# One core, attention into a spectral MLP: a searched order of work and loads, and DMA transposes for part of x and u

## The chip, the cores and the metric

The kernel runs on 1 core of one Trainium2 chip. The metric is device microseconds of one execution; the span of the profile is about 2 us shorter than the time. There is one core, so the state of a run is judged by its time alone: a run more than 1.5% above the fastest of the same kernel counts as slow and is left out of a ratio.

## The reference

Eight batches of chunked attention (8 heads, 576 positions, head size 64, softmax within chunks of 64) give x; then a gated token mixer and a residual MLP. Cut to what matters:

```python
scores = q_c @ k_c.T / 8                 # per chunk of 64
attn = softmax(scores)                   # within the chunk
x = (attn @ v_c)                         # [8, 576, 512], heads side by side
theta = x @ w_theta
y = w_tok_r @ (x * cos(theta)) + w_tok_i @ (x * sin(theta))   # over positions
u = x + y
out = u + relu(u @ w_ch)                 # float32
```

## The kernel before

Batches go in pairs (p = 0 to 3), each of 9 tiles of 128 positions, in 5 groups g of two tiles (group 2, the middle one, has one). Everything is emitted in an order written down as a list of items: `a1` turns q and k, `a2` scores and exp, `a3` attention times v and division, `a4` turns x, `a5` theta with cos and sin, `z` their products with x, `y` the token product (one per batch and 128 channels, plus the residual x, which gives u transposed, `uT`), `w` the last product, `st` the final sum and the store. Each engine does its instructions in that order.

```python
def a4(p, g, bits):                       # x -> xT, on TensorE
    ps = psum2("ps_xT", FP16)
    ...
    for jj in range(n):
        for db in range(NDB):             # NDB = 4
            nc.tensor.transpose(psv[:, db, jj*P : jj*P+P],
                                st[p]["x", g][:, jj, db*P : db*P+P], id16)
    ...                                   # then one copy PSUM -> xT on DVE or ACT

def w(p, j):
    for db in range(NDB):
        nc.tensor.matmul(ps[:, 0:DM], uT[:, db, j*P : j*P+P], wch16[:, db, :], ...)
        nc.tensor.matmul(ps[:, DM+db*P : DM+db*P+P],     # u turned back
                         uT[:, db, j*P : j*P+P], id16)
    nc.scalar.activation(out=r, in_=ps[:, 0:DM], func=AF.Relu)

def out_tile(p, j):
    nc.vector.tensor_tensor(out=o, in0=ps[:, DM : 2*DM], in1=r, op=ALU.add)
    nc.sync.dma_start(out[...], o[...])
...
# loads: on GpSimd's queue, each as soon as its buffer's last reader has been emitted
```

PSUM is one ring of four buffers; a tile of `w` holds one until its `st`.

The softmax here doesn't subtract the row's maximum and nothing guards it: scores larger than these inputs give would overflow.

Of the kernel before, what the change touches and what calls it, by code (L numbers as in the profile page):

```python
# [9 lines left out]
FP32 = mybir.dt.float32  # L10
FP16 = mybir.dt.float16
# [38 lines left out]


# [1 line left out]
def kernel(  # L53
# [27 lines left out]
    GROUPS = [(0, 2), (2, 2), (4, 1), (5, 2), (7, 2)]  # L81
    VP = D + 2
    NAT = 7

    const = ctx.enter_context(tc.tile_pool(name="const", bufs=1))
    glob = ctx.enter_context(tc.tile_pool(name="glob", bufs=1))
# [102 lines left out]
            nc.gpsimd.dma_start(wnat[hf][ri][0:CH, 2, :], ap[KT * P : S, :])  # L189

    def load_w(ap, f16):
        nc.gpsimd.dma_start(f16, ap.rearrange("(a p) e -> p a e", p=P))


# [143 lines left out]
            op=ALU.mult,  # L338
        )

    def a4(p, g, bits):

        j0, n = GROUPS[g]
        ps = psum2("ps_xT", FP16)
        psv = ps[:, 0 : NDB * n * P].rearrange("p (a s) -> p a s", a=NDB)
        for jj in range(n):
            for db in range(NDB):
                nc.tensor.transpose(  # L348
                    psv[:, db, jj * P : jj * P + P],
                    st[p]["x", g][:, jj, db * P : db * P + P],  # L350
                    id16,
                )
# [12 lines left out]

    def a5(p, g):

# [99 lines left out]
            op=ALU.add,  # L467
        )

    def w(p, j):  # L470

        uT = uT_tile(p)
        ps = psum2("ps_uw")
        for db in range(NDB):
            nc.tensor.matmul(  # L475
                ps[:, 0:DM],
                uT[:, db, j * P : j * P + P],
                wch16[:, db, :],
                start=(db == 0),
                stop=(db == NDB - 1),  # L480
            )
            nc.tensor.matmul(  # L482
                ps[:, DM + db * P : DM + db * P + P],
                uT[:, db, j * P : j * P + P],
                id16,
            )
        r = outp.tile([P, DM], FP32, name="relu", bufs=3)
        nc.scalar.activation(out=r, in_=ps[:, 0:DM], func=AF.Relu)  # L488
        st[p]["w", j] = (ps, r)

    def out_tile(p, j):
        ps, r = st[p].pop(("w", j))
        o = outp.tile([P, DM], FP32, name="o32")
        nc.vector.tensor_tensor(out=o, in0=ps[:, DM : 2 * DM], in1=r, op=ALU.add)  # L494
# [52 lines left out]
_INS = ['q', 'k', 'v', 'moe_w_theta', 'moe_w_tok_r', 'moe_w_tok_i', 'moe_w_ch']  # L547
# [26 lines left out]
```

## Time and profile before

| | before |
|---|---|
| time, median of 4 runs | 219.27 us (218.46 to 222.02) |
| span of the profile | 217.4 us |
| TensorE / VectorE / ScalarE / GpSimd busy | 91 / 61 / 54 / 39% |
| first theta matmul; end of the last matmul | 21.75; 213.1 us |
| TensorE busy between these two | 188.5 of 191.4 us |
| after the last matmul | 4.3 us |

In the lines below, PEld is TensorE's loading of weights, and SPq and POOLq are the DMA issues of SP (SyncE) and GpSimd. A row of a stage gives the stretch, its length, then busy microseconds (and instructions) of PE, PEld, DVE, ACT and POOL, the granted clock of TensorE, the share of the DMA engines and GB/s. Busy time of matmuls overlaps, so the cost of one in a stream is read from the distance of two starts. The lines that carry this are in the prediction.

### The profile page before, as it was taken

How to read it: one execution, taken by the hardware profiler on the slowest of the kernel's cores; microseconds unless marked ns; L12 is line 12 of the kernel's file. 1: busy time of each engine (PE TensorE's matmuls, PEld its weight loads, DVE VectorE, ACT ScalarE, POOL GpSimd, SP SyncE). 2: the span in 40 equal slices, each digit the busy share in tenths (PEclk: the TensorE clock that was granted, in tenths of full speed). 3: DMA queues.
4: the chain of work that ended last, by engine and by line, in shares of the span. 5: the costliest groups of instructions: out<-in, count | busy, mean ns of one | idle time of the engine just before them, and what ended most of it. 6: DMA issues, size and time to landing. Idle time of an engine off the chain costs nothing.

```text
span 217.4 us, 6721 instructions
## 1 busy us (share of the span) xinstructions
PE 198.8 (91%) x2994; PEld 138.8 (64%) x2994; DVE 132.8 (61%) x230; ACT 118.5 (54%) x138; POOL 85.1 (39%) x118
## 2 busy tenths in 40 slices
PE   0485999989999999999997999999999999999992
PEld 0374568765677875667886664776766675777750
DVE  0148486747977575869776837567836655275273
ACT  2244484338968689838574468753085446321242
POOL 7896468679885698765920000000000000000000
PEclk9999999999999999999999999999999999999999
DMA  6999999999999999999990012112121313113136
GB/s 59 177 131 166 200 181 179 177 170 132 166 221 196 165 132 181 213 228 192 142 164 5 3 48 72 51 51 48 53 96 51 121 48 100 48 49 147 48 124 216
DMA packets 83612, 26.92 MB, mean 124 GB/s; under 512 B 76288, under 2 KB 78976, under 8 KB 83584
## 3 DMA queue, kind: packets, MB, share of 16 engines
q0 software_dynamic: 77696, 16.54, 86.0%
q1 hardware_dynamic: 5888, 9.96, 13.5%
q8 instruction: 23, 0.38, 0.7%
q14 instruction: 5, 0.04, 0.0%
HBM read 33.06 MB, written 9.44 MB: 195 GB/s over the span
## 4 chain that ended last, share of the span: by engine, by line
PE 80%; DMA 6%; DVE 4%; POOL 3%; issue 3%; ACT 2%; POOLq 0%
PE ps_y L455 28%; PE ps_theta L377 14%; PE ps_uw L475 13%; PE ps_qkT L266 6%; PE ps_y L434 4%; PE ps_sT L292 4%; DMA wtheta<-in_moe_w_theta_dram 3%; PE ps_uw L482 3%; PE ps_xT L348 3%; PE ps_x L320 3%; DMA qk<-in_k_dram 3%; POOL v L176 2%; PE ps_wT L218 1%; POOL qk L155 1%; DVE o L494 1%
## 5 line engine op out<-in xcount | busy, mean ns | idle before, releaser
L455 PE MATMUL ps_y<-wT,z 128*128 128x288 f16 x448 | 59.8, 286 | 1.2 <-issue 1.2
L455 PEld LDWEIGHTS <-z 128*128 128x128 f16 x448 | 42.2, 98 | 13.8 <-issue 1.5
L176 POOL DMA_DIRECT2D v<-in_v_dram x56 | 42.0, 766 | 17.3 <-DMA qk<-in_k_dram 10.7
L475 PE MATMUL ps_uw<-wch,uT 128*128 128x512 f16 x144 | 42.5, 380 | 0.0
L488 ACT ACTIVATE relu<-ps_uw 128x512 f32<-128x512 f32 x36 | 21.6, 600 | 37.6 <-PE ps_uw L482 37.2
L463 DVE TENSOR_TENSOR uT<-ps_y,xT 128x576 f16<-128x576 f32 x28 | 21.2, 755 | 28.8 <-PE ps_y L455 28.7
L494 DVE TENSOR_TENSOR o<-ps_uw,relu 128x512 f32<-128x512 f32 x36 | 24.5, 686 | 11.7 <-ACT relu L488 11.5
L482 PE MATMUL ps_uw<-id,uT 128*128 128x128 f16 x144 | 31.5, 219 | 0.0
L377 PE MATMUL ps_theta<-wtheta,xT 128*128 128x512 f16 x128 | 30.5, 384 | 0.1
L266 PE MATMUL ps_qkT<-id,qk 128*64 128x128 f16 (+1 forms) x640 | 22.5, 227 | 6.4 <-DMA qk<-in_q_dram 5.7
L387 ACT ACTIVATE cos<-ps_theta,pihalf 128x1024 f16<-128x1024 f32 (+1 forms) x20 | 20.6, 1029 | 12.7 <-PE ps_theta L377 12.4
L334 DVE TENSOR_TENSOR x<-ps_x,recip 128x512 f16<-128x512 f32 x36 | 24.9, 691 | 1.2
L266 PEld LDWEIGHTS <-qk 128*64 128x64 f16 (+1 forms) x640 | 19.1, 118 | 8.8 <-DMA qk<-in_q_dram 5.7
L299 ACT ACTIVATE eT<-ps_sT 128x1024 f16<-128x1024 f32 (+1 forms) x20 | 18.3, 940 | 11.4 <-PE ps_sT L292 11.4
L475 PEld LDWEIGHTS <-uT 128*128 128x128 f16 x144 | 14.1, 98 | 14.7
L197 DVE COPY kT<-ps_qkT 128x1024 f16<-128x1024 f16 (+1 forms) x13 | 15.2, 1169 | 12.5 <-ACT qT L199 12.5
L155 POOL DMA_DIRECT2D qk<-in_k_dram x24 | 19.1, 797 | 5.5 <-DMA qk<-in_q_dram 2.9
L377 PEld LDWEIGHTS <-xT 128*128 128x128 f16 x128 | 12.1, 99 | 13.6 <-issue 0.9
L155 POOL DMA_DIRECT2D qk<-in_q_dram x24 | 19.3, 805 | 2.1 <-POOLq L558 0.8
L391 ACT ACTIVATE sin<-ps_theta 128x1024 f16<-128x1024 f32 (+1 forms) x20 | 18.7, 933 | 0.0
L199 ACT COPY kT<-ps_qkT 128x1024 f16<-128x1024 f16 (+1 forms) x7 | 8.4, 1224 | 14.2 <-DVE qT L197 14.2
L292 PE MATMUL ps_sT<-qT,kT 64*64 64x64 f16 x576 | 12.3, 223 | 3.9 <-ACT kT L199 2.9
(51 smaller groups left out, 212.0 us busy)
## 6 DMA issues: line engine op xcount, KB each, us to landing
out_dram<-o SPq DMA_DIRECT2D x32, 256.0 KB, 2.1
qk<-in_q_dram POOLq DMA_DIRECT2D x16, 256.0 KB, 6.9
qk<-in_k_dram POOLq DMA_DIRECT2D x16, 256.0 KB, 8.2
v<-in_v_dram POOLq DMA_DIRECT2D x40, 64.0 KB, 6.4
v<-in_v_dram POOLq DMA_DIRECT2D x16, 128.0 KB, 6.3
out_dram<-o SPq DMA_DIRECT2D x8, 128.0 KB, 2.9
wnat<-in_moe_w_tok_r_dram POOLq DMA_DIRECT2D x2, 288.0 KB, 8.9
wnat<-in_moe_w_tok_i_dram POOLq DMA_DIRECT2D x2, 288.0 KB, 9.6
```

The costliest lines, as they stand in the source:

```text
L155: nc.gpsimd.dma_start(t[(pp // 2) : (pp // 2) + m // 2, ti].rearrange("p h t d -> p h (t d)"), src.rearrange("h (p t) d -> p h (t d)", t=2),)
L176: nc.gpsimd.dma_start(v16[pp : pp + m, sl, :, 0:D], v[2 * p + bb, :, s0 : s0 + m, :].rearrange("h s d -> s h d"),)
L266: nc.tensor.transpose(psv[par * D : par * D + D, w, e, tk, 0:rows], t[0:rows, w, 2 * e + par, tk, :], id16[0:rows, 0:rows],)
L292: nc.tensor.matmul(psv[kh * CH : kh * CH + CH, par, i, e, :], kT[par * D : par * D + D, e, c0 : c0 + CH], qT[par * D : par * D + D, e, c0 ...
L334: nc.vector.tensor_tensor(out=xo, in0=px[:, :, :, 0:D], in1=recip.broadcast_to((P, 2, NE, D)), op=ALU.mult,)
L377: nc.tensor.matmul(ps[:, jj * DM : jj * DM + DM], xt[:, db, :], wtheta16[:, db, :], start=(db == 0), stop=(db == NDB - 1),)
L455: nc.tensor.matmul(psv[:, hf, 0:HS], zt[:, db * P : db * P + P], wT[:, kt, hf * HS : hf * HS + HS], start=(kt == 0), stop=(kt == 2 * KT),)
L463: nc.vector.tensor_tensor(out=uT_tile(p)[:, db, sl].rearrange("p (f c) -> p f c", f=2), in0=psv[:, :, 0:HS], in1=xT_tile(p)[:, db, sl].rea ...
L475: nc.tensor.matmul(ps[:, 0:DM], uT[:, db, j * P : j * P + P], wch16[:, db, :], start=(db == 0), stop=(db == NDB - 1),)
L482: nc.tensor.matmul(ps[:, DM + db * P : DM + db * P + P], uT[:, db, j * P : j * P + P], id16,)
L488: nc.scalar.activation(out=r, in_=ps[:, 0:DM], func=AF.Relu)
L494: nc.vector.tensor_tensor(out=o, in0=ps[:, DM : 2 * DM], in1=r, op=ALU.add)
```

## The change

Its intent: TensorE is the bound, and the DMA engines are four fifths idle once the loads are done, so turn there what can be turned by DMA, and search an order of all work, loads and choices of engine that fits. The core of the diff, the list of items left out (the two comment lines at its end say in words what it does there; KT is 4: tiles 0 to 3 of a pair go with its first batch, 4 to 8 with its second):

```diff
+    U_DMA = 3
...
+    def xt(p, g):
...
+        for jj in range(n):
+            c0 = x_col(j0 + jj)
+            nc.sync.dma_start_transpose(xT[:, :, c0 : c0 + P], x[:, jj, :])
...
     def a4(p, g, bits):
+        if bits & 16:
+            xt(p, g)
+            if n == 1:
+                xm_copy(p, bits >> 1)
+            return
...
+    def ut(p, bb, db):
+        cols = slice(KT * P, T) if bb else slice(0, KT * P)
+        nc.sync.dma_start_transpose(
+            un_tile(p, bb)[:, :, db * P : db * P + P], uT_tile(p)[:, db, cols]
+        )
...
     def w(p, j):
-            nc.tensor.matmul(ps[:, DM + db * P : DM + db * P + P], uT[...], id16)
-        nc.scalar.activation(out=r, in_=ps[:, 0:DM], func=AF.Relu)
+            if 2 * p + int(j >= KT) < U_DMA:
+                nc.tensor.matmul(ps[:, DM + db * P : DM + db * P + P], uT[...], id16)
+        if 2 * p + int(j >= KT) < U_DMA:
+            nc.scalar.activation(out=r, in_=ps[:, 0:DM], func=AF.Relu)
...
     def out_tile(p, j, bits):
+        else:
+            nc.vector.scalar_tensor_tensor(out=o, in0=ps[:, 0:DM], scalar=0.0,
+                in1=un_tile(p, int(j >= KT))[...], op0=ALU.max, op1=ALU.add)
+        eng = nc.gpsimd if bits & 2 else nc.sync
...
-    # loads issued by a rule between the items
+    # loads are items of the order (lq, lv, lw, lt, lc)
```

The 33 transposes (13 of x in the last 7 groups, 20 of u of the last five batches) all go through SP's queue; 18 of the 36 tiles are stored from GpSimd's queue instead of SP's.

More of the change, by code (lines that the diff above doesn't have):

```diff
@@ L19 @@
 ORDER = """
-a1.0.0:0 a2.0.0:0 a1.0.1:3 a1.0.2:2 a3.0.0.0:0 a2.0.1:0 a3.0.0.1:0 a2.0.2:0 a3.0.2.0:0
-a4.0.0:1 a4.0.2:3 a3.0.1.0:0 a3.0.1.1:0 a5.0.2:0 a4.0.1:1 a5.0.0:0 z.0.2.0:0 z.0.0.0:0
-tw.0.1:0 tw.1.0:0 a5.0.1:0 z.0.0.1:0 tw.0.2:0 tw.1.1:0 z.0.1.0:0 z.0.1.1:0 tw.0.0:1
-tw.1.2:0 a1.0.3:2 yh.0.0:0 a2.0.3:0 yh.0.1:0 a1.0.4:3 a3.0.3.0:0 yh.1.0:0 a3.0.3.1:0
-a2.0.4:0 yh.1.1:0 a3.0.4.0:0 a1.1.0:0 a4.0.3:0 w.0.0:0 a2.1.0:0 a3.0.4.1:0 st.0.0:0
-a5.0.3:0 a4.0.4:1 a1.1.1:2 z.0.3.0:0 a5.0.4:0 a3.1.0.0:0 w.0.1:0 z.0.4.0:0 a1.1.2:0
@@ L26 @@
-st.0.1:0 z.0.3.1:0 w.0.2:0 st.0.2:0 a3.1.0.1:0 a2.1.1:0 z.0.4.1:0 a1.1.3:3 w.0.3:0
-a4.1.0:1 st.0.3:0 y.0.1.0:0 a2.1.2:0 a2.1.3:0 a3.1.1.0:0 a5.1.0:0 a3.1.3.0:0 a1.1.4:2
-y.0.1.1:0 a3.1.2.0:0 a2.1.4:0 y.0.1.2:0 a4.1.2:0 a1.2.0:1 a3.1.1.1:0 a1.2.1:0 z.1.0.0:0
-y.0.1.3:0 a4.1.1:0 a3.1.4.0:0 a2.2.1:0 a2.2.0:0 a3.1.3.1:0 w.0.4:0 z.1.0.1:0 a5.1.2:0
-st.0.4:0 a4.1.3:1 w.0.5:0 a5.1.1:0 st.0.5:0 a3.1.4.1:0 a1.2.2:3 z.1.2.0:0 a5.1.3:0
-z.1.1.0:0 w.0.6:0 a4.1.4:1 w.0.7:0 st.0.6:0 st.0.7:0 a1.2.3:3 z.1.1.1:0 a3.2.1.0:0
@@ L32 @@
-a1.2.4:0 w.0.8:0 a5.1.4:0 st.0.8:0 y.1.0.0:0 a2.2.2:0 a2.2.3:0 z.1.4.0:0 a3.2.1.1:0
-z.1.3.0:0 z.1.3.1:0 y.1.0.1:0 a3.2.2.0:0 a2.2.4:0 a1.3.0:3 z.1.4.1:0 y.1.0.2:0 a4.2.1:1
-a4.2.2:0 a1.3.1:1 a3.2.0.0:0 a3.2.4.0:0 y.1.1.0:0 a1.3.2:3 a2.3.0:0 a3.2.0.1:0 a1.3.3:3
-a2.3.1:0 a3.3.0.0:0 y.1.0.3:0 a4.2.0:0 a3.2.3.0:0 a1.3.4:3 a3.2.3.1:0 a3.2.4.1:0
-y.1.1.1:0 w.1.0:0 st.1.0:0 a4.2.3:0 a4.2.4:1 a5.2.0:0 y.1.1.2:0 w.1.1:0 a5.2.2:0
-z.2.0.0:0 a5.2.1:0 st.1.1:0 z.2.2.0:0 z.2.0.1:0 w.1.2:0 a5.2.3:0 z.2.1.0:0 z.2.1.1:0
@@ L38 @@
-st.1.2:0 a5.2.4:0 y.1.1.3:0 w.1.3:0 a2.3.2:0 z.2.3.0:0 z.2.3.1:0 st.1.3:0 a3.3.1.0:0
-y.2.0.0:0 z.2.4.0:0 a2.3.3:0 a3.3.1.1:0 a2.3.4:0 y.2.0.1:0 a4.3.1:0 w.1.4:0 z.2.4.1:0
-a3.3.0.1:0 st.1.4:0 a3.3.4.0:0 y.2.0.2:0 w.1.5:0 a3.3.4.1:0 st.1.5:0 a3.3.3.0:0
-y.2.1.0:0 a3.3.3.1:0 a3.3.2.0:0 y.2.1.1:0 w.1.6:0 a4.3.2:3 w.1.7:0 st.1.6:0 a5.3.2:0
-w.1.8:0 st.1.7:0 y.2.0.3:0 st.1.8:0 a5.3.1:0 w.2.0:0 a4.3.0:1 z.3.1.0:0 st.2.0:0 w.2.1:0
-st.2.1:0 z.3.1.1:0 y.2.1.2:0 a5.3.0:0 w.2.2:0 z.3.2.0:0 a4.3.4:0 st.2.2:0 z.3.0.0:0
@@ L44 @@
-z.3.0.1:0 y.2.1.3:0 a4.3.3:0 w.2.3:0 y.3.0.0:0 w.2.4:0 st.2.3:0 st.2.4:0 a5.3.4:0
-a5.3.3:0 w.2.5:0 z.3.4.0:0 z.3.4.1:0 st.2.5:0 y.3.0.1:0 w.2.6:0 y.3.0.2:0 z.3.3.0:0
-w.2.7:0 st.2.6:0 z.3.3.1:0 y.3.0.3:0 st.2.7:0 w.2.8:0 y.3.1.0:0 w.3.0:0 st.2.8:0
-st.3.0:0 y.3.1.1:0 w.3.1:0 y.3.1.2:0 st.3.1:0 w.3.2:0 y.3.1.3:0 st.3.2:0 w.3.3:0 w.3.4:0
-w.3.5:0 st.3.3:0 st.3.4:0 w.3.6:0 w.3.7:0 st.3.5:0 w.3.8:0 st.3.6:0 st.3.7:0 st.3.8:0
+lq.0.0:0 a1.0.0:2 lq.0.2:0 a1.0.2:2 lq.0.1:0 a2.0.0:0 a2.0.2:0 a1.0.1:3 lv.0.2:0
@@ new lines @@
+lv.0.0:0 a3.0.0.0:0 a3.0.2.0:0 a2.0.1:0 a3.0.0.1:0 lv.0.1:0 a3.0.1.0:0 lw.0:0 lq.0.3:0
+a3.0.1.1:0 a4.0.0:1 a4.0.2:0 lq.0.4:0 a4.0.1:1 a5.0.2:0 lt.0.1:0 z.0.2.0:0 a5.0.0:0
+lt.0.0:0 z.0.0.0:0 a1.0.3:3 a5.0.1:0 lq.1.0:0 a1.0.4:0 z.0.1.0:0 lv.0.4:0 tw.0.2:0
+tw.0.0:0 z.0.1.1:0 lt.1.0:0 z.0.0.1:0 tw.0.1:0 a2.0.3:0 lt.1.1:0 a2.0.4:0 lv.0.3:0
+lv.1.0:0 a1.1.0:2 yh.0.0:0 lq.1.2:0 a3.0.4.0:0 a2.1.0:0 a3.0.4.1:0 yh.0.1:0 a4.0.4:1
+lc.0:0 tw.1.1:0 tw.1.2:1 tw.1.0:1 a3.0.3.0:0 lq.1.1:0 a3.0.3.1:0 a5.0.4:0 lv.1.2:0
@@ new lines @@
+a4.0.3:1 yh.1.0:0 lq.1.3:0 a5.0.3:0 z.0.4.0:0 lq.1.4:0 a3.1.0.0:0 z.0.3.0:0 a1.1.2:2
+yh.1.1:0 z.0.3.1:0 z.0.4.1:0 a2.1.2:0 lv.1.3:0 a3.1.0.1:0 a1.1.1:3 lv.1.1:0 w.0.0:0
+st.0.0:0 y.0.1.0:0 a3.1.2.0:0 a1.1.3:0 lq.2.0:0 w.0.1:0 lv.1.4:0 a4.1.2:1 st.0.1:0
+y.0.1.1:0 a2.1.3:0 a1.1.4:3 a2.1.1:0 a3.1.3.0:0 lq.2.2:0 w.0.2:0 st.0.2:0 y.0.1.2:0
+a2.1.4:0 a3.1.3.1:0 a4.1.0:1 a5.1.2:0 lv.3.0:0 a3.1.1.0:0 a1.2.0:2 a5.1.0:0 lq.2.1:0
+lv.2.2:0 a3.1.4.0:0 lv.2.0:0 a3.1.1.1:0 y.0.1.3:0 a4.1.1:1 a3.1.4.1:0 z.1.0.0:0 a1.2.2:1
@@ new lines @@
+w.0.3:0 st.0.3:0 a4.1.3:1 a4.1.4:0 lq.2.3:0 z.1.2.0:0 a5.1.1:0 w.0.4:0 a5.1.4:0 st.0.4:2
+w.0.5:0 lq.2.4:0 z.1.1.0:0 z.1.0.1:0 z.1.4.0:0 a5.1.3:0 st.0.5:0 z.1.1.1:0 a2.2.0:0
+a1.2.1:2 y.1.0.0:0 lv.2.1:0 a1.2.3:1 a3.2.0.0:0 lv.2.4:0 z.1.3.0:0 a2.2.2:0 y.1.0.1:0
+z.1.3.1:0 a2.2.1:0 lv.3.2:0 a3.2.2.0:0 a1.2.4:0 w.0.6:0 st.0.6:0 a4.2.2:1 lv.2.3:0
+y.1.0.2:0 w.0.7:0 z.1.4.1:0 a3.2.0.1:0 lq.3.0:0 a2.2.4:0 st.0.7:2 lv.3.4:0 y.1.0.3:0
+a3.2.1.0:0 a3.2.4.0:0 y.1.1.0:0 a4.2.0:0 a3.2.4.1:0 a1.3.0:3 a2.2.3:0 lq.3.2:0
@@ new lines @@
+a3.2.1.1:0 w.0.8:0 lq.3.1:0 lq.3.3:0 a5.2.2:0 a4.2.1:0 lv.3.3:0 w.1.0:0 lq.3.4:0
+st.0.8:0 lv.3.1:0 z.2.2.0:0 st.1.0:0 y.1.1.1:0 a5.2.1:0 w.1.1:0 st.1.1:2 a5.2.0:0
+z.2.1.0:0 z.2.0.0:0 y.1.1.2:0 a3.2.3.0:0 a1.3.2:0 z.2.1.1:0 a2.3.0:0 a1.3.1:0 z.2.0.1:0
+w.1.2:0 st.1.2:0 y.1.1.3:0 y.2.0.0:0 ut.1.1.0:0 a2.3.2:0 ut.1.1.3:0 a3.3.0.0:0 a1.3.3:0
+a3.2.3.1:0 y.2.0.1:0 a4.2.4:16 a4.2.3:17 a2.3.1:0 a3.3.0.1:0 a1.3.4:0 a2.3.3:0
+a3.3.1.0:0 ut.1.1.2:0 y.2.0.2:0 a3.3.1.1:0 a4.3.0:17 a2.3.4:0 ut.2.0.1:0 ut.1.1.1:0
@@ new lines @@
+a3.3.3.0:0 a5.2.3:0 w.1.3:0 a5.2.4:0 st.1.3:2 y.2.0.3:0 z.2.3.0:0 w.1.4:0 a4.3.1:17
+a5.3.0:0 z.2.3.1:0 st.1.4:2 z.2.4.0:0 z.2.4.1:0 w.1.5:0 st.1.5:2 z.3.0.0:0 a5.3.1:0
+w.1.6:0 st.1.6:0 y.2.1.0:0 a3.3.4.0:0 a3.3.2.0:0 ut.2.0.0:0 ut.2.0.2:0 y.2.1.1:0
+a3.3.4.1:0 a3.3.3.1:0 z.3.1.0:0 w.1.7:0 st.1.7:2 y.2.1.2:0 ut.2.0.3:0 w.1.8:0 a4.3.2:18
+a5.3.2:0 a4.3.3:17 z.3.0.1:0 a4.3.4:17 st.1.8:2 w.2.0:0 st.2.0:2 z.3.2.0:0 z.3.1.1:0
+y.2.1.3:0 a5.3.3:0 z.3.3.0:0 w.2.1:0 ut.2.1.1:0 ut.2.1.3:0 a5.3.4:0 st.2.1:0 w.2.2:0
@@ L49 @@
+ut.2.1.0:0 ut.2.1.2:0 st.2.2:2 y.3.0.0:0 w.2.3:0 st.2.3:2 y.3.0.1:0 w.2.4:0 st.2.4:2
+y.3.0.2:0 z.3.3.1:0 ut.3.0.1:0 ut.3.0.2:0 ut.3.0.0:0 w.2.5:0 z.3.4.0:0 z.3.4.1:0
+st.2.5:0 y.3.0.3:0 w.2.6:0 ut.3.0.3:0 st.2.6:2 y.3.1.0:0 w.2.7:0 st.2.7:0 y.3.1.1:0
+w.2.8:0 st.2.8:2 ut.3.1.1:0 ut.3.1.0:0 y.3.1.2:0 w.3.0:0 st.3.0:2 y.3.1.3:0 w.3.1:0
+st.3.1:2 w.3.2:0 w.3.3:0 ut.3.1.2:0 ut.3.1.3:0 w.3.4:0 st.3.2:0 st.3.3:2 st.3.4:0
+w.3.5:0 st.3.5:0 w.3.6:0 st.3.6:0 w.3.7:0 w.3.8:0 st.3.7:0 st.3.8:2
 """.split()
@@ L339, in a3, with xm_copy @@
         )
+    def xt(p, g):
+        j0, n = GROUPS[g]
+        x = st[p]["x", g]
+        xT = xT_tile(p)
+        if n == 1:
+            xm = trig.tile([P, NDB, P], FP16, name="xTm", bufs=1)
+            st[p]["xTm"] = xm
+            nc.sync.dma_start_transpose(xm, x[:, 0, :])
+            return
+        for jj in range(n):
+            c0 = x_col(j0 + jj)
+            nc.sync.dma_start_transpose(xT[:, :, c0 : c0 + P], x[:, jj, :])
+    def xm_copy(p, bits):
+        copy(
+            not bits & 1,
+            xT_tile(p).rearrange("p a (b s) -> p a b s", b=2)[:, :, :, KT * P : S],
+            st[p]["xTm"].rearrange("p a (b s) -> p a b s", b=2),
+        )
     def a4(p, g, bits):
         j0, n = GROUPS[g]
+        if bits & 16:
+            xt(p, g)
+            if n == 1:
+                xm_copy(p, bits >> 1)
+            return
         ps = psum2("ps_xT", FP16)
@@ L359, in a4 @@
         copy(bits & 1, xm, psv)
-        copy(
-            not bits & 2,
-            xT.rearrange("p a (b s) -> p a b s", b=2)[:, :, :, KT * P : S],
-            xm.rearrange("p a (b s) -> p a b s", b=2),
-        )
+        xm_copy(p, bits >> 1)
     def a5(p, g):
@@ L468, in y, with un_tile @@
         )
+    def un_tile(p, bb):
+        return once(p, ("un", bb), lambda: pairp.tile(
+            [P, KT + bb, DM], FP16, name=f"un{bb}", bufs=1))
+    def ut(p, bb, db):
+        cols = slice(KT * P, T) if bb else slice(0, KT * P)
+        nc.sync.dma_start_transpose(
+            un_tile(p, bb)[:, :, db * P : db * P + P], uT_tile(p)[:, db, cols]
+        )
     def w(p, j):
@@ L481, in w @@
             )
-            nc.tensor.matmul(
-                ps[:, DM + db * P : DM + db * P + P],
-                uT[:, db, j * P : j * P + P],
-                id16,
-            )
-        r = outp.tile([P, DM], FP32, name="relu", bufs=3)
-        nc.scalar.activation(out=r, in_=ps[:, 0:DM], func=AF.Relu)
+            if 2 * p + int(j >= KT) < U_DMA:
+                nc.tensor.matmul(
+                    ps[:, DM + db * P : DM + db * P + P],
+                    uT[:, db, j * P : j * P + P],
+                    id16,
+                )
@@ L489, in w, with out_tile @@
+        r = None
+        if 2 * p + int(j >= KT) < U_DMA:
+            r = outp.tile([P, DM], FP32, name="relu", bufs=3)
+            nc.scalar.activation(out=r, in_=ps[:, 0:DM], func=AF.Relu)
         st[p]["w", j] = (ps, r)
-    def out_tile(p, j):
+    def out_tile(p, j, bits):
         ps, r = st[p].pop(("w", j))
         o = outp.tile([P, DM], FP32, name="o32")
-        nc.vector.tensor_tensor(out=o, in0=ps[:, DM : 2 * DM], in1=r, op=ALU.add)
-        for pp, bb, s0, n in out_ranges(j):
-            nc.sync.dma_start(out[2 * p + bb, s0 : s0 + n, :], o[pp : pp + n])
@@ L499 @@
-    BATCH = [[0, 1, 2], [3, 4]]
-    LOADS = [(p, g) for p in range(NP) for g in BATCH[0] + BATCH[1]]
-    def load(i):
-        load_qk(*LOADS[i])
-        load_v(*LOADS[i])
-    load_qk(*LOADS[0])
-    make_identity(nc, id16)
-    for i in (1, 2):
-        load_qk(*LOADS[i])
-    for i in range(3):
-        load_v(*LOADS[i])
-    load_w(moe_w_theta, wtheta16)
-    for hf in range(2):
-        for ri in range(2):
-            load_tok_w(hf, ri)
-    for i in (3, 4):
-        load(i)
-    load_w(moe_w_ch, wch16)
@@ L519 @@
-    for i in range(5, NAT):
-        load(i)
-    loaded = NAT
-    seen = set()
+        if 2 * p + int(j >= KT) < U_DMA:
+            nc.vector.tensor_tensor(out=o, in0=ps[:, DM : 2 * DM], in1=r, op=ALU.add)
+        else:
+            nc.vector.scalar_tensor_tensor(
+                out=o,
+                in0=ps[:, 0:DM],
+                scalar=0.0,
+                in1=un_tile(p, int(j >= KT))[:, j % KT if j < KT else j - KT],
+                op0=ALU.max,
+                op1=ALU.add,
+            )
@@ L523 @@
+        eng = nc.gpsimd if bits & 2 else nc.sync
+        for pp, bb, s0, n in out_ranges(j):
+            eng.dma_start(out[2 * p + bb, s0 : s0 + n, :], o[pp : pp + n])
     emit = dict(a1=a1, a2=a2, a3=a3, a4=a4, a5=a5, z=z, y=y, yh=yh, w=w,
-                st=out_tile, tw=tw)
-    for item in ORDER:
+                st=out_tile, tw=tw, ut=ut, lq=load_qk, lv=load_v, lt=load_tok_w,
+                lw=lambda _: load_w(moe_w_theta, wtheta16),
+                lc=lambda _: load_w(moe_w_ch, wch16))
@@ L526 @@
+    for n, item in enumerate(ORDER):
         name, bits = item.split(":")
@@ L528 @@
         args = [int(i) for i in args]
-        if kind in ("a1", "a4", "tw"):
-            emit[kind](*args, int(bits))
-        else:
-            emit[kind](*args)
-        seen.add(name)
-        while loaded < len(LOADS):
-            p, g = LOADS[loaded]
-            pn, gn = LOADS[loaded - NAT]
-            need = {f"a1.{pn}.{gn}"}
-            if p >= 2:
-                need |= {f"a3.{p - 2}.{g}.{hg}" for hg in range(GROUPS[g][1])}
-            if not need <= seen:
-                break
-            load(loaded)
-            loaded += 1
+        if kind in ("a1", "a4", "tw", "st"):
+            args.append(int(bits))
+        emit[kind](*args)
+        if n == 0:
+            make_identity(nc, id16)
 _INS = ['q', 'k', 'v', 'moe_w_theta', 'moe_w_tok_r', 'moe_w_tok_i', 'moe_w_ch']
```

## The prediction

> **What bounds the kernel now.** I read the page's busy shares first, then the busy times by stage, the chain of work that ended last, and last the timeline of the final stage for the true spacing of matmuls. On the page:
>
> ```profile
> PE 198.8 (91%) x2994; PEld 138.8 (64%) x2994; DVE 132.8 (61%) x230; ACT 118.5 (54%) x138; POOL 85.1 (39%) x118
> ...
> DMA  6999999999999999999990012112121313113136
> ```
>
> TensorE (PE) is at 91%, no other engine above 61%. The DMA row has two halves: saturated until slice 21 (115 us), where the loads end, then one to three tenths. By stage (columns: stretch, its length, then busy us of PE, PEld, DVE, ACT, POOL; granted clock; DMA share; GB/s):
>
> ```profile
> 0.00:21.75 21.75, 10.28 (x269) 8.44 (x269) 7.94 (x18) 7.40 (x8) 18.07 (x30) 1.00 1.38 133
> 21.75:50.00 28.25, 27.41 (x426) 18.79 (x427) 17.46 (x31) 14.04 (x16) 19.41 (x26) 1.00 1.79 178
> ...
> 86.00:120.00 34.00, 32.02 (x691) 24.31 (x690) 25.18 (x44) 22.35 (x26) 18.18 (x25) 1.00 1.52 157
> 120.00:206.59 86.59, 86.55 (x840) 58.45 (x839) 50.31 (x86) 41.38 (x53) 0.00 (x0) 1.00 0.19 65
> ```
>
> Up to 21.75 us PE starves: that is when w_theta lands and the first theta matmul starts. From there PE is short of work for 0.8 us before 50 and 2.0 us between 86 and 120, and from 120 to 206.6 it is never idle (86.55 of 86.59), while the DMA engines are 19% busy. The chain agrees: 80% of it is PE, and these pieces of it (start, length, what) show the startup, the cadence and the end:
>
> ```profile
> 14.16 7.46 DMA wtheta<-in_moe_w_theta_dram
> 21.75 1.87 PE ps_theta L377 x4
> ...
> 175.27 0.45 PE ps_xT L348 x8
> 176.80 2.21 PE ps_y L455 x18
> ...
> 213.15 0.60 ACT relu L488
> 213.77 0.69 DVE o L494
> ```
>
> "Busy" of a pipelined matmul is not what it costs the stream. The group table gives the 128x128 identity matmul of u 219 ns; the timeline gives its cost by the starts:
>
> ```profile
> 203.35 0.22 PE L482 MATMUL ps_uw<-id,uT 128*128 128x128 f16 x1
> ...
> 203.41 0.38 PE L475 MATMUL ps_uw<-wch,uT 128*128 128x512 f16 x1
> ...
> 203.62 0.22 PE L482 MATMUL ps_uw<-id,uT 128*128 128x128 f16 x1
> ...
> 203.68 0.38 PE L475 MATMUL ps_uw<-wch,uT 128*128 128x512 f16 x1
> ```
>
> After an identity matmul starts, the next one follows 0.055 to 0.06 us later; after a w_ch matmul, 0.21 to 0.22 us. So one tile of w costs PE 4 x 0.273 = 1.09 us, of which 0.22 is turning u back. A transpose of x costs 0.45/8 = 0.056 us.
>
> **What the Trainium skill says.** "VectorE: DVE Perf Modes", section "The three transpose paths", gives 390 ns for a 128x128 transpose on TensorE and 1309 ns by the DMA crossbar. The trace has 219 to 232 ns for the first, and 0.056 us of it as cost in a full stream; the second is not in this trace. "DMA: Bandwidth & Descriptors", section "Latency and other measured facts", gives 261 GB/s for a DMA transpose with a non-contiguous middle dimension. The same page, section "Rules for kernel authors", says that a plain DMA transpose is issued from SP or ACT, that two streams of them must not overlap, and that one beside ordinary DMAs needs nothing: here all are on SP, one stream. Its section "Issuing engines are not separate DMA queues" says that all issuers share the 16 DMA engines; the trace shows these full for the first half and four fifths free after it, which is why the transposes are put there.
>
> **The change, part by part.**
>
> 1. u of five batches (second batch of pair 1, both of pairs 2 and 3: 5 + 9 + 9 = 23 tiles) loses its identity matmuls: 23 x 4 = 92 x 0.055 = **5.1 us of PE**. All of these tiles run after y of pair 1, so in the stage where PE has no idle: the whole of it should count.
> 2. x of the last 7 groups (six of 8 transposes, one of 4: 52) leaves PE: 52 x 0.056 = **2.9 us of PE**, in the same stage. Also off PE's road: seven PSUM copies on DVE or ACT (0.6 to 1.0 us each), and seven uses of the four PSUM buffers.
> 3. The 23 relus on ACT (0.60 us each, 13.8 us) go; DVE does max and add in one instruction from PSUM (as now 128x512 from f32 PSUM, so I take the 0.69 us of the present add). Off the path, but for the end: the last tile's relu, **0.6 us**.
> 4. Added: 20 transposes of u (8 of four and 12 of five 128x128 blocks) and 13 of x (four blocks), 33 in SP's queue, 144 blocks or 4.7 MB; about half of the stores move to GpSimd's queue, so that SP is free. The last store goes there too: a GpSimd issue takes about 0.8 us on the page against 0.34 for SP's, so +0.4 us.
> 5. The order. Before w_theta the same q, k and v pieces are loaded (groups 0, 1, 2), so it should land at about 21.7 us again; the first three a4 and three a5 wait behind it as now. Then groups 3 and 4 go ahead of the token weights. Adding up PE's items with durations as in the chain (y 2.21, w 1.09 or 0.87, theta of two tiles 1.73, q/k transposes 1.01, scores 1.0, one half group of x 0.25, x turned 0.45), PE's work is 197.5 us before and 189.6 us after, of which 7.0 and 7.4 are done before the first theta. Check on the kernel before: 21.75 - 7.0 + 197.5 = 212.3, against 213.1 where its last matmul ends, so about 0.8 us more than the sum. I give the order 0.5 us, since some of the 2.8 us of idle could go; I can't read more from this trace.
>
> Sum: 5.1 + 2.9 + 0.6 - 0.4 + 0.5 = 8.7 us, giving 210.7 if every transpose lands before it is needed.
>
> **Are the transposes in time?** SP works them in order. The first that must wait for something late is u's last quarter of pair 1 (after the last y of pair 1, at PE work 113.8 us); from there to the end 32 transposes share 189.6 - 113.8 = 76 us: **2.4 us each** on average. The tightest stretch: from that y (u is ready about 0.9 us later, at 114.7) to the theta of group 1 of the last pair at PE work 137.7, 11 transposes are queued: 23.0/11 = **2.1 us each**. At the end, the last quarter of u is ready about 0.9 us after the last y (work 182.6), so at 183.5; the five last tiles then need 5 x 0.69 = 3.5 us of DVE, while PE ends at 189.6: the last transpose may take some 2.5 to 3 us to land before it shows. Estimates of one transpose's hold on the queue: by bytes at the skill's 261 GB/s, 128 KB takes 0.5 us; by its 1309 ns per block without overlap, four blocks take 5.2 us. The plain SBUF-to-SBUF copies of 64 KB in SP's queue now take 0.5 us to issue and 3.8 us to land, in good part while DMA is full. I take 1.3 to 2 us, because the order was searched and its spacing fits about 2 us, and charge 0.6 us for waits left over. That is a choice, not a reading. 210.7 + 0.6 = **211.3 us**.
>
> **Rivals.** (a) SP's queue becomes the bound: if a transpose holds it for over about 2.4 us, theta of the last pair waits on x, DVE's final add waits on u, and PE follows through the four PSUM buffers. At 2.6 us, 32 x 2.6 = 83 us instead of 76 makes +7 us and eats the gain (about 218); at the unoverlapped 5.2 us, 32 x 5.2 = 166 us makes +90 us. For it: the page's 1309 ns; against it: DMA is 19% busy, and a tuned order would hardly have kept such a queue. (b) The load phase gives something back: the token weights come later, GpSimd's queue now has stores (which wait for DVE) among loads, and DMA is full there: up to 3 us of PE idle around 25 to 60 us, so about 214. For it: the 2.8 us idle that the present order has; against it: the work before the first token product also grows, from groups 3 and 4. (c) A clean win with a better startup: if PE's remaining 2.8 us of idle go and the transposes are hidden, 211.3 - 2.3 - 0.6 = about 208.4. (d) The removed matmuls were free, because another engine paces the late stage: against it DVE 50 and ACT 41 us in 86.6; then there would be no change, but I give that little.
>
> **Range and chances.** The low end is (c), 208; the high end allows (b) or an average transpose near 2.4 us with some 4 us of waits, 216. Within 2% means above 215.1, which takes waits of 4.4 us over the clean sum: 0.13. Slower by 2% (over 223.8) takes (a) with more than 2.7 us each: 0.05. The runs of before spread over 218.5 to 222.0, which adds about a microsecond either way.
>
> **What will show it.** Right: identity matmuls fall from 144 to 52, PE work after the first theta is about 182 us, w tiles late in the span start 0.87 us apart, w_theta again lands near 21.7 us, relu x13, transposes landing in 2 to 3 us with SP waiting for DVE rather than the other way. Wrong: PE or PEld waits released by a DMA of xT, DVE's final add released by a DMA of un, growing gaps before theta of the last pair, an idle tail of more than 5 us after the last matmul, or PE idle between 25 and 60 us.

## The result, and the profile after

The changed kernel takes 212.13 us (211.16 to 212.75, 4 runs) against 219.27 us: ratio 0.968, 95% interval 0.962 to 0.974. A ratio here is the mean time of one kernel's fast runs over that of the other's from the same rounds, so not quite the ratio of the medians. The prediction was 211.3 us.

The page of the changed kernel, its row of busy times and its DMA row (40 slices of 5.3 us):

```profile
PE 190.6 (90%) x2850; PEld 130.8 (62%) x2850; DVE 131.7 (63%) x230; ACT 97.4 (46%) x106; POOL 96.7 (46%) x139
...
DMA  5999999999999993999999996665354796462883
```

144 matmuls are gone and TensorE is still at 90%. The last load lands at 126.7 us instead of 115.3, and after that the DMA engines are about half busy instead of a fifth. By stage of the changed kernel, and then cut at the first theta and the last matmul:

```profile
86.00:120.00 34.00, 33.82 (x562) 24.26 (x551) 22.47 (x41) 21.93 (x25) 24.32 (x33) 1.00 1.54 150
120.00:150.00 30.00, 28.10 (x520) 19.73 (x519) 15.48 (x30) 17.76 (x19) 2.01 (x3) 0.94 0.86 123
...
21.84:204.63 182.79, 179.66 (x2576) 121.39 (x2574) 121.94 (x211) 91.73 (x100) 75.88 (x107) 0.99 1.18 151
204.63:210.70 6.07, 0.00 (x1) 0.00 (x0) 0.69 (x1) 0.00 (x0) 0.54 (x1) 0.67 0.43 165
```

The first theta starts where it did (21.84 against 21.75 us). From there to the last matmul it takes 182.8 us instead of 191.4, 8.6 less. The tail grew from 4.3 to 6.1 us, 1.8 more. Together with the 0.1 at the start that is the 6.7 us by which the span fell (217.4 to 210.7).

The idle of 2.0 us between 86 and 120 has gone, but there is a new one of 1.9 us between 120 and 150. The chain of work that ended last shows it (start, length, what), and the stages of 2 us around it show what follows:

```profile
135.95 0.70 DVE x L345
136.65 0.47 SPq L364
137.17 4.49 DMA xT<-x
141.71 1.83 PE ps_theta L410 x4
143.54 0.43 PE ps_uw L519
```

```profile
140.00:142.00 2.00, 0.29 (x1) 0.11 (x2) 0.41 (x1) 1.06 (x1) 0.00 (x0) 0.95 0.94 58
142.00:144.00 2.00, 2.00 (x7) 0.85 (x6) 0.00 (x0) 0.42 (x1) 0.00 (x0) 0.50 0.49 101
144.00:146.00 2.00, 2.00 (x11) 0.89 (x9) 0.00 (x0) 2.00 (x3) 0.00 (x0) 0.70 0.47 96
```

The first group turned by DMA whose theta comes (group 3 of pair 2) waits at its second tile for that tile's transpose. TensorE stands 1.9 us, and then its clock is granted at 0.50 and 0.70 for four microseconds: a 512-column matmul that started 0.22 us after the one before now takes 0.43 us. That costs another 2 x 0.50 + 2 x 0.30 = 1.6 us, so the wait is worth about 3.5 us. The Trainium skill, "TensorE: Matmul & The Clock Gate", section "What's actually happening", has the mechanism: the array runs at half rate after an idle window of some 3.4 us, measured on a free-running window, and at full rate after a busy one. The trace agrees on half rate and on the length: the clock is 0.50 for 3.4 us, from 141.8 to 145.2. It does not agree on the idle time before it: 1.9 us here, and 2.1 us in the profiled run of the tail's edits below. Nor does idle time of that length always bring half rate: after 2.0 us at 29 us in the last run of this text, and after 3.0 us at 182 in the one with every transpose twice, the clock stayed at 1.00.

The transposes themselves in the changed kernel: issues (count, median us from issue to landing), the durations of the issue on SP's queue (minimum, median, maximum in ns), and SP's queue from 115 us on:

```profile
un<-uT SPq DMA_TRANSPOSE x20, 3.3
...
xT<-x SPq DMA_TRANSPOSE x12, 3.2
```

```profile
L364 SPq DMA_TRANSPOSE xT<-x x12: 1188/1262/2185, 132.3 to 167.1; - x12
```

```profile
115.03 13.97 SPq L554 DMA_DIRECT2D out_dram<-o  x2
129.05 3.17 SPq L510 DMA_TRANSPOSE un<-uT  x2
132.27 6.16 SPq L364 DMA_TRANSPOSE xT<-x  x4
```

A transpose of x holds the queue for 1.26 us and lands 3.2 us after its issue, in the median. The second row of the queue starts at 129: SP had a store ahead of it, which waits for a sum on DVE until 128.6 us. Behind it come two transposes of u, then the four of x, of which the last is issued at 137.2 and lands at 141.7, 4.5 us later, while its theta could have begun at about 139.8. The chain names a product x on DVE before this issue, but that one belongs to pair 3, and the queue has no gap above 0.1 us from 129.05 to 138.4: what the issue waited for is its turn.

### The profile page after: what moved, and what is told of

It is laid out like the page before. It is cut to its first block, busy times and chain, and to the rows that moved or that the text cites. A ratio compares the mean times of both kernels' runs of the same rounds, so it can differ in the third digit from the quotient of the medians.

```text
span 210.7 us, 6454 instructions
## 1 busy us (share of the span) xinstructions
PE 190.6 (90%) x2850; PEld 130.8 (62%) x2850; DVE 131.7 (63%) x230; ACT 97.4 (46%) x106; POOL 96.7 (46%) x139
## 4 chain that ended last, share of the span: by engine, by line
PE 64%; issue 11%; POOL 10%; DMA 8%; ACT 2%; DVE 2%; POOLq 0%; SPq 0%
PE ps_y L488 22%; PE ps_theta L410 12%; PE ps_uw L519 9%; DMA qk<-in_k_dram 6%; PE ps_qkT L277 6%; POOL qk L165 5%; PE ps_y L467 4%; PE ps_sT L303 3%; POOL v L186 3%; PE ps_x L331 3%; DMA xT<-x 2%; PE ps_xT L385 2%; POOL out_dram L554 2%; PE ps_uw L527 1%; ACT qT L210 1%
## 5 line engine op out<-in xcount | busy, mean ns | idle before, releaser
L554 POOL DMA_DIRECT2D out_dram<-o x21 | 11.5, 550 | 89.4 <-DVE o L544 50.3
L488 PEld LDWEIGHTS <-z 128*128 128x128 f16 x448 | 43.0, 98 | 14.0 <-issue 0.2
L519 PE MATMUL ps_uw<-wch,uT 128*128 128x512 f16 x144 | 39.0, 386 | 0.0
L410 PE MATMUL ps_theta<-wtheta,xT 128*128 128x512 f16 x128 | 31.2, 386 | 1.9 <-DMA xT<-x 1.9
L542 DVE TENSOR_TENSOR o<-ps_uw,relu 128x512 f32<-128x512 f32 x13 | 8.9, 687 | 16.4 <-ACT relu L535 16.3
L544 DVE SCALAR_TENSOR_TENSOR o<-ps_uw,un 128x512 f32<-128x512 f32 x23 | 15.9, 689 | 5.2 <-PE ps_uw L519 3.6
L208 DVE COPY kT<-ps_qkT 128x1024 f16<-128x1024 f16 (+1 forms) x11 | 13.1, 1191 | 7.5 <-ACT qT L210 7.5
L210 ACT COPY kT<-ps_qkT 128x1024 f16<-128x1024 f16 (+1 forms) x9 | 10.6, 1181 | 9.5 <-DVE qT L208 9.5
L331 PE MATMUL ps_x<-v,eT 64*64 64x65 f16 x576 | 11.4, 200 | 3.4 <-DMA v<-in_v_dram 2.5
```

What stands on the lines that cost most here:

```text
L331: nc.tensor.matmul(psv[half * CH : half * CH + CH, kh if n == 2 else f0, cols], eT[kh * CH : kh * CH + CH, i, h // 2, h % 2, :], v16[kh * ...
L410: nc.tensor.matmul(ps[:, jj * DM : jj * DM + DM], xt[:, db, :], wtheta16[:, db, :], start=(db == 0), stop=(db == NDB - 1),)
L488: nc.tensor.matmul(psv[:, hf, 0:HS], zt[:, db * P : db * P + P], wT[:, kt, hf * HS : hf * HS + HS], start=(kt == 0), stop=(kt == 2 * KT),)
L519: nc.tensor.matmul(ps[:, 0:DM], uT[:, db, j * P : j * P + P], wch16[:, db, :], start=(db == 0), stop=(db == NDB - 1),)
```

## The experiments

All runs gave correct results. Times are medians; that of the kernel before is given with each call. The four runs of the first call came from one chip, so did the four of the second and the three of the third.

### First call (before: 218.9 us): the parts one at a time

**The changed kernel again.** It was run six more times, on the chip of the other runs of this call.

> The changed kernel unaltered, so that all of this call is compared on one chip: 212 us, 0.968 of the kernel before. In its trace the first theta of a group turned by DMA (group 3 of pair 2, near 139 us) should again find PE idle for about 2 us, released by a DMA of xT.

Measured: 209.44, 209.67, 210.63, 213.47, 213.77, 213.81 us, ratio 0.959 for the fast three (the others are over 1.5% above the fastest). The profiled run, 209.44 us, has no wait of TensorE for xT: PE is busy 30.00 of 30.00 us between 120 and 150, where the profiled run of the result had 28.10. So the expectation of a wait in it fell: the same kernel runs with it or without. The distance fits the 3.5 us estimated above, but up to here a state of the chip would explain it as well. (The four runs of the result, 211.2 to 212.8 us, lie between the two kinds; one of them has a trace.) SP's queue was no earlier in the run without the wait: the store left at 129.1 us instead of 128.7, and the last of the four xT was issued at 137.6 instead of 137.2. But it landed 2.5 us later and not 4.5. That one transpose, in the result's run and in this one (tile xT, windows 137.2:137.5 and 137.7:137.9):

```profile
L364 SPq DMA_TRANSPOSE xT<-x x1: 1265/1265/1265, 137.2 to 137.2; - x1
...
DMA to landing us min/median/max: 4.5/4.5/4.5
```

```profile
L364 SPq DMA_TRANSPOSE xT<-x x1: 1275/1275/1275, 137.6 to 137.6; - x1
...
DMA to landing us min/median/max: 2.5/2.5/2.5
```

So these two runs differ in a landing, and the queue decides whether there is room for the long one. What makes a landing long or short is not shown.

**The order alone.**

```diff
-    U_DMA = 3
+    U_DMA = 99          # u by TensorE for all tiles; the ut items taken out
-a4.2.4:16 a4.2.3:17 a4.3.0:17 ...
+a4.2.4:0  a4.2.3:1  a4.3.0:1  ...   # x by TensorE for all groups
```

> The new order, loads and store queues, but x and u turned by TensorE as before. Theory A (all of the gain is the 144 matmuls taken off PE, the order gives nothing): as the kernel before, 219 us. Theory B (the order itself removed the idle of PE in the load phase, and part of what the transposes freed was lost again to the wait for xT and to the tail): 216 to 217 us, and PE idle between 21.75 and 120 us about 1 us instead of 2.8.

Measured: 219.51 us, ratio 1.003 (1.001 to 1.006). Theory A. TensorE's idle between 21.75 and 120 us did fall, to 1.1 + 0.1 + 0.2 us, as theory B said, but between 150 and 180 us it now stands 1.3 us, for example here, where theta of the middle group follows its own transposes at once:

```profile
166.04 1.04 PE L410 MATMUL ps_theta<-wtheta,xTm 128*128 128x512 f16 x4 [0.94 <-ACT xTm L210]
```

Its tail after the last matmul is 6.1 us as well, so the longer tail comes with the new list (its last store is GpSimd's) and not with the transposes. The order is made for transposes elsewhere, and by itself it is no better than the old one.

**u by DMA, x on TensorE** (only the `a4` bits as above).

> u by DMA, x back on TensorE (52 transposes, +2.9 us of PE work against the changed kernel). Theory A (x's part counts in full): 215 us. Theory B (x's part is eaten by the wait of about 2 us for xT and the half-speed clock after it): 211.5 to 213 us, with no PE idle near 139 us and the clock at full speed there.

Measured: 214.49 us, ratio 0.981 (0.978 to 0.984). Theory A, near its 215 us. Against the order alone that is 5.0 us less, which is the 5.1 us of the identity matmuls. There is no wait near 139 us.

**x by DMA, u on TensorE** (only `U_DMA` and the `ut` items as above).

> x by DMA, u back on TensorE (92 identity matmuls, +5.1 us of PE work against the changed kernel, and the relus on ACT). Both theories: u's part counts in full but for the tail, 216 to 217.5 us. If it is below 215, u's part was mostly lost to something else, the burst of stores at the end above all. The wait for xT should shrink, as three transposes of u ahead of it in SP's queue are gone: PE idle near 139 us under 1 us.

Measured: 214.48 us, ratio 0.980 (0.978 to 0.983). Below the expected 216 to 217.5, but not for the reason named there. Against the order alone it is again 5.0 us less, while 52 transposes are worth 2.9: the idle of 1.3 us between 150 and 180 went as well (30.00 of 30.00 busy). That makes 4.2; the other 0.8 us are not explained. With the u transposes out of the queue, PE did not wait for xT in its profiled run.

In runs without the wait the parts add up: 219.5 - 5.0 - 5.0 = 209.5, and the changed kernel's fast kind is 209.4 to 210.6 us.

### Second call (before: 219.66 us): the wait, the tail, the queue

**One store off SP's queue.**

```diff
-w.1.2:0 st.1.2:0 y.1.1.3:0
+w.1.2:0 st.1.2:2 y.1.1.3:0      # 2: store from GpSimd's queue
```

> The changed kernel with one store (tile 2 of pair 1) moved from SP's to GpSimd's queue. The changed kernel showed two kinds of runs in one call, 209.4 to 210.6 and 213.5 to 213.8 us. Theory: the slow kind is the wait of the first late theta for the fourth xT transpose (PE idle 1.9 us at 139.8, then half clock), and the transposes start late because this store holds SP until 128.6 us, waiting for DVE. Then all runs lie at 209 to 210.6, none at 213, and the first u transpose starts near 121 us instead of 129. Rival: the two kinds are a state of the chip (clock), and then they stay, 209.5 and 213.5, in about equal parts.

Measured: 209.30, 213.62, 210.99, 209.32, 210.26, 209.09 us; ratio of the fast 0.955. Five of six are of the fast kind, one is not. The first u transpose did move, to 115.8 us, and in the profiled run the last of the four xT is issued at 135.2 us instead of 137.2. More was not to be had from this edit: the second u transpose, still ahead of x, left only at 129.7 us, when DVE had made its data. The edit helps but the expectation of no run at 213 missed, so this run did not settle it.

**The tail.**

```diff
-st.3.7:0 st.3.8:2
+st.3.7:0 st.3.8:0               # last store from SP's queue
-        o = outp.tile([P, DM], FP32, name="o32")             # 4 buffers
+        o = outp.tile([P, DM], FP32, name="o32", bufs=5)
```

> The changed kernel with the last store on SP's instead of GpSimd's queue, and 5 instead of 4 output buffers. After the last matmul the changed kernel takes about 6 us, the kernel before 4.3; of it 0.7 us is DVE waiting for an output buffer, 0.3 + 0.5 us GpSimd's issue. Theory: 1.0 to 1.3 us shorter tail. Rival: the stores of the last tiles are bound by the DMA engines (0.95 busy there), then the last store lands when it did and under 0.4 us comes of it. The two kinds of runs stay as they are.

Measured: 208.57 to 212.10 us, median 211.25, ratio of the fast 0.957. The spread hides the size, as expected; the next run shows it. The profiled run, a slow one of 212.1 us, is the second trace with the wait: 2.1 us of TensorE for xT, whose last transpose was issued at 138.6 us and took 4.3 to land.

**Both edits.**

> Both edits. Theory: all runs at 208.2 to 209.6 us. If the store on SP was not the cause of the slow kind, some runs stay near 212.5.

Measured: 207.79 us (207.32 to 208.31), ratio 0.946 (0.943 to 0.949). All six runs are within 0.5%, below the 208.2 to 209.6 us expected, the fastest kernel. The two edits of the tail are worth 2.0 us of median against the run with the store alone. Cut at the last matmul, the tail of the run with the store alone and of this one:

```profile
201.27:207.30 6.03, 0.00 (x0) 0.00 (x0) 0.69 (x1) 0.00 (x0) 0.54 (x1) 0.69 0.43 165
```

```profile
201.58:205.90 4.32, 0.01 (x1) 0.00 (x0) 0.69 (x1) 0.00 (x0) 0.00 (x0) 1.00 0.61 231
```

The tail is 4.3 us again, as before the change, so the 1.8 us go with the output buffers and the queue of the last store; with the rival, that the load of the DMA engines bounds the last stores, under 0.4 us would have come of it. The tail is not the old one, though: the last sum ends 0.7 us after the last matmul instead of 1.4, as no relu stands between, and from there to the end it takes 3.6 us instead of 2.9. The cause of these 0.7 us is not shown. No run has one of the edits alone; by the traces, the last sum on DVE ends 4.8 us before the span does in the changed kernel (205.9 to 210.7) and 3.6 us with SP's store (202.3 to 205.9), which is 1.2 us for the queue, and DVE's wait of 0.7 us for an output buffer is down to the usual 0.2.

**Every transpose twice**, the second into a spare tile.

```diff
             nc.sync.dma_start_transpose(xT[:, :, c0 : c0 + P], x[:, jj, :])
+            again(x[:, jj, :], NDB)        # same source, two spare buffers in turn
```

> The changed kernel with every transpose issued a second time, into a spare tile that nobody reads. Each holds SP's queue for 1.27 us (median of the trace), so the 33 hold it 42 us of the 72 between the first and the last; twice that is 84 us. Theory (the queue is the resource that bounds transposes, rival (a) of the prediction): waits of PE for xT and of DVE for un appear and the time rises by 12 to 25 us, to 222 to 235. Rival (SP's hold is only issue and the queue is not near its limit): under 5 us more.

Measured: 245.27 us (245.1 to 246.1), ratio 1.118. That is 33 us over the changed kernel, above even the range of the theory. The waits of this run (engine, line, released by: us in all, times, longest):

```profile
PE ps_theta L417 <- DMA xT<-x: 16.3, 7, 5.6
...
DVE o L552 <- DMA un<-uT: 11.6, 2, 7.8
```

With issues of 1.27 us in the median as before, the 66 transposes hold SP's queue for 91 of the 104 us from the first to the last: the queue has become the bound. The DMA engines have not: their share is 0.90 and 0.54 from 120 to 150 and to 180 us, 0.86 and 0.62 in the changed kernel. The longest waits bring half clock too (0.78 in the mean between 150 and 180 us), which the theory had left out. So the queue had room for 33 transposes and not for 66; rival (a) of the prediction was real and the change is on the right side of it, the one wait at 139.8 us apart.

### Third call (before: 219.65 us): earlier, more, and the old order

**The two transposes of group 4 earlier**, on top of both edits.

```diff
-w.1.2:0 st.1.2:2 ... y.2.0.1:0 a4.2.4:16 a4.2.3:17
+w.1.2:0 a4.2.4:16 st.1.2:2 ... y.2.0.1:0 a4.2.3:17
```

> The kernel of the run st12_tail (207.8 us) with the two transposes of x of group 4, pair 2 (ready since about 106 us) put ahead of the u transposes in SP's queue. Theory: the fourth xT transpose then lands about 2 us ahead of its theta instead of at it, so no run can fall into the slow kind: all at 207.3 to 208.3 us, no gain in the median. Rival: transposes issued while the loads still run take much longer to land (8.1 us was seen for the one that st12_tail issues at 115.8 us, 2.4 to 4.5 after the loads), and delay those behind them: 209 to 212 us.

Measured: 208.32 us (207.09 to 209.24), ratio 0.950 (0.944 to 0.955). No wait for xT, no gain over the run before it, as expected; the runs lie 1 us wider than said.

**Two more groups by DMA, while the loads run**, on top of that (`a4.2.0` and `a4.2.1` with bit 16).

> early_x24 with x of two more groups (0 and 1 of pair 2) turned by DMA, between 100 and 115 us, while the loads still fill the DMA engines. TensorE loses 16 more transposes, 0.9 us. Theory A (the skill's statement that a transpose beside ordinary DMAs needs nothing, taken for time as well): 207 us. Theory B (landing takes 6 to 9 us there, and their thetas come 4 to 10 us after x is ready): PE waits for xT, 1 to 6 us, and 209 to 213 us.

Measured: 215.16 us (212.68 to 216.56), ratio of the fast 0.975 (0.968 to 0.983): worse by more than theory B said. The fast runs alone show it, 212.7 to 215.6 us against 207.1 to 209.2. The profile happened to be of one of the slow runs (215.9 us), so the size of its wait is that run's only:

```profile
119.58 1.89 PE L410 MATMUL ps_theta<-wtheta,xT 128*128 128x512 f16 x4 [6.34 <-DMA xT<-x]
```

The longest landing of an xT is 10.7 us there, against 4.7 in the changed kernel. Saving 0.9 us of TensorE beside the loads costs about 7.

**The old order with the DMA transposes**: the list, loads and stores of the kernel before, with the same 7 groups and five batches by DMA, each u transpose as early as its data and its one buffer allow.

> The order, loads and stores of the kernel before, with x of the same 7 groups and u of the same five batches by DMA (each u transpose put as early as its data and its single buffer allow). Since the new order alone gave nothing (219.5 us): theory A, the order is worth nothing with DMA either: 209.5 to 212 us. Theory B, the searched order is what gives each transpose its 5 to 8 us before its theta: in the old one four groups of the last pair have theta 1 to 7 us behind x, so PE waits 2 to 4 us at several of them: 214 to 222 us.

Measured: 218.50 us (217.51 to 219.29), ratio 0.996 (0.991 to 1.001). Theory B: the same transposes that are worth 9 to 10 us in the new order, in runs without the wait, are worth 1 in the old. It is one placing by hand, and all stores stay on SP's queue; that a better placing in the old order would give more is not excluded. TensorE waits for x turned by DMA at four places, 3.6 us in all, the longest:

```profile
169.44 3.56 PE L410 MATMUL ps_theta<-wtheta,xT 128*128 128x512 f16 x8 [2.18 <-DMA xT<-x]
```

PE is busy 27.26 of 30 us between 150 and 180 at a clock of 0.94, and 6.1 us of tail follow the last matmul.

### Fourth call (before: 219.97 us): the wait alone

**The two transposes of group 4 earlier, in the changed kernel**, nothing else: the item `a4.2.4:16` stands before `st.1.2:0`.

> The changed kernel with one item moved: the two transposes of x of group 4, pair 2 ahead of the store of tile 2, pair 1, in SP's queue. Nothing else is changed, neither the tail nor which queue stores use. Theory (the spread of the changed kernel, 209.4 to 213.8 us, comes from the fourth xT transpose landing just before or just after its theta): all six runs at 209.0 to 210.6 us, no PE wait for xT in the trace. Rival (the spread is the chip's): about half of the runs at 211 to 214.

Measured: 210.09, 209.58, 208.93, 209.92, 209.88, 209.47 us, ratio 0.951 (0.947 to 0.955). All six are of the fast kind. SP's queue in its trace:

```profile
116.63 3.15 SPq L364 DMA_TRANSPOSE xT<-x  x2
129.87 0.35 SPq L554 DMA_DIRECT2D out_dram<-o  x1
130.27 3.23 SPq L510 DMA_TRANSPOSE un<-uT  x2
133.60 2.52 SPq L364 DMA_TRANSPOSE xT<-x  x2
```

Two transposes pass in the time in which SP used to wait, and the last xT is issued at 134.9 us, though the store came no earlier (129.9 us). It takes 4.4 us to land, as long as in the run with the wait, and at 139.2 us is in time. The theory held: the changed kernel's spread (209.4 to 213.8 us) came from one transpose that lands just before or just after it is needed. The chip was another than in the first call, so that the chip has no part in it isn't shown; but on the chip of the first call both kinds appeared, and the edited order shows one kind on each of two chips.

## Why the prediction was right

The time (211.3 predicted, 212.1 measured) and the class are right, and by its steps:

1. **u, 5.1 us: right.** u by DMA against the order alone: 5.0 us. Late w tiles start 0.86 us apart in the chain of the changed kernel; 0.87 was said.
2. **x, 2.9 us: too small.** Measured 5.0 us against the order alone. Of the 2.1 us more, 1.3 are idle of TensorE behind its own x transposes between 150 and 180 us, which the new order brought; 0.8 are not explained.
3. **The relu at the end, -0.6, and GpSimd's last store, +0.4: wrong in sign.** Together -0.2 us was charged, and the tail grew by 1.8 us. The step priced only the issue of GpSimd's store, where the way from the last sum to the end is 1.2 us longer than with SP's, and it did not look at the output buffers: the relu's 0.6 us was right, but DVE's wait for a buffer took its place. Two edits brought the tail back to 4.3 us.
4. **The order, 0.5 us: of another kind than the step assumed.** Alone, with its tail, it gives nothing (1.003). Yet without it the transposes give 0.4% (0.996). The prediction's sum treated order and transposes as terms to be added; they are not. What the order brings is the time between the issue of a transpose and its reader. The line "the whole of it should count", because TensorE has no idle there, is true only of an order that leaves that time.
5. **Transposes in time, 0.6 us left: the right place, too small in the runs of the result.** The guess of 1.3 to 2 us of queue per transpose holds: 1.26 us in the median, 1.4 in the mean. The tightest stretch was named, from the last y of pair 1 to the theta of group 1 of the last pair, and the wait fell inside it, at the first theta and not the last. The working shared the stretch among its transposes (11 by its count, 12 in the list) and did not ask at each theta on the way: up to the first one there are 10.7 us (129.1 to 139.8) for six issues and a landing of up to 4.5 us. It also overlooked the store that held SP until 128.6 us, which put one more transpose, 1.4 us, into this stretch; with the store moved away the four of x start 1.3 us earlier. The wait costs 1.9 us and then 1.6 us of half clock, which the prediction did not have.

So the time was met by terms that cancel. The tail took 2.0 us more than charged, and the wait 2.0 (the median of 212.1 lies 2.6 above the 209.5 of runs without it); x gave 2.1 more, and the order without its tail some 0.7 more (219.5 - 218.9 - 1.8 = -1.2, where -0.5 was charged). That makes 1.2 where 0.8 was measured, as near as these differences are known. Two of the signs by which the prediction wanted to be found wrong did appear, the wait of TensorE for a DMA of xT and a tail above 5 us. Of the rivals, (a) is real at twice the transposes; (b) did not happen, the load phase lost nothing (0.95 us idle from 21.75 to 50, 0.8 before, up to 2.0 in later runs; and 0.2 instead of 2.0 from 86 to 120); (c), about 208.4, is where the kernel with three small edits came out, 207.8 us; (d) is refuted by the run with u alone.

## What to carry to other kernels

Work moved from the bound engine to a queue is worth its full time only if every item is issued its landing time ahead of its reader, so count the whole in-order queue up to that item, stores that wait for something included. An order searched for one assignment of work was worth nothing here for another (219.5 against 218.9 us): test the two together, and each alone. If a kernel's own runs fall into two kinds, look for a transfer that lands just at its reader before blaming the chip; moving it by one place tests it.

## What the Trainium skill lacked or had wrong

- "VectorE: DVE Perf Modes", section "The three transpose paths", has 1309 ns for a 128x128 block by DMA. Here one transpose of four or five such blocks, SBUF to SBUF, holds SP's queue for 1.26 us and lands after 3.2 to 3.3 us (median); four times the page's figure, 5.2 us, would have been four times the hold.
- "DMA: Bandwidth & Descriptors", section "Latency and other measured facts", has 261 GB/s for a DMA transpose. 128 KB in a hold of 1.26 us is 104 GB/s, back to back in one queue. For such a transpose on trn2 no page has the time for which it holds the issuing queue (the same page counts a sequencer's cycles per transpose for other shapes, where it compares trn3 with what came before).
- The same page, section "Rules for kernel authors", says that a transpose next to ordinary DMAs needs nothing. The results were correct, as it says; but none says that beside saturated loads the landing takes up to 10.7 us, against 2.4 to 4.7 after them.
- "TensorE: Matmul & The Clock Gate", section "What's actually happening", gives an idle window of about 3.4 us for the drop to half rate. Stands of 1.9 and 2.1 us were followed by one here (granted clock 0.50 for 3.4 us), stands of 2.0 and 3.0 us in other runs were not: no run shows a length that decides.
